# A fused attention and two-MLP kernel: a tile of ones is multiplied on TensorE behind the first q transposes and behind six score groups of pair 0

## The chip, the core and the metric

The kernel runs on one NeuronCore of one Trainium2 chip, in one launch. The metric is the device time of an execution in microseconds (us). Before the change three runs took 1049.36, 1034.11 and 1044.68 us, so their median is 1044.68 us. One more execution was profiled: it took 1044.74 us, and the span from its first to its last instruction is 1043.0 us, so 1.74 us lie outside what the trace shows.

## What is computed

In float32: attention over 4 batches and 8 heads with 576 positions of 64 numbers, then two feed-forward blocks over the 2304 resulting rows of 512.

```python
q_rot, k_rot = (rotate(q), rotate(k))            # rotary embedding, halves of 32
scores = scale * np.matmul(q_rot, k_rot.transpose(0, 1, 3, 2))
attn = np.exp(scores - np.max(scores, axis=-1, keepdims=True))
attn = attn / (np.sum(attn, axis=-1, keepdims=True) + 1e-09)
x = np.matmul(attn, v)                           # heads side by side: 2304 x 512
h = x @ w_in;  x = (h - np.tanh(h)) @ w_out      # 512 -> 2048 -> 512
x = ((x @ w1) * (x @ w2)) @ w3 @ w_o2            # 512 -> 1024 -> 1024 -> 512
```

## The kernel before, in words

**Pairs and steps.** Attention goes in 16 pairs of heads (4 batches x 4 pairs). A pair's q, k and v are loaded for two heads side by side, so that one 128x128 transpose serves both. Of the 576 positions, 512 are four chunks of 128, and the last 64 of both heads make a fifth chunk, the tails. So a pair has nine score groups (step S0 for the tails, S1 to S8 for four chunks x two heads), each a 128x576 tile.

**A score group's way through the engines.** TensorE multiplies a group (`score`, L535, PSUM tile `sc`, of which there are two buffers). VectorE takes the negated maximum of each row (`top`, L540, `nm`). ScalarE writes the exponentials with their sums (`exps`, L545, `e`), and that frees the `sc` buffer. VectorE inverts the sums, GpSimd divides (`norm`, L565), TensorE transposes the result in blocks (`trans`, L593 and L596, PSUM tile `te`), ScalarE and VectorE evict it (`eta`, `etb`, `ett`), and `pv` (L631, L634) multiplies with v.

**Before the scores of a pair** TensorE transposes the rotated k (`prep_k`, step KT, L454, `tk`), the tails (`prep_t`, TT, L460, `tt`) and q (`prep_q`, QT, L417, `tq`). ScalarE and VectorE split each into a rounded high part and the rest (`kp`: steps K1, K2, E1, ES; `qp`: Q1, Q2; `qtd`: G and H). For pair 0 the score matmuls read `kp` and `qp` in place: three terms for each half of the columns, six matmuls of 288 columns a group, whose operands fill 64 of 128 partitions; only S0 fills 128. For later pairs the SP queue copies `kp` and `qp` into stacked tiles `ks` and `qs` first (`twice_k` L504, steps KD0 to KD3, and `twice_q` L448, QD0 to QD3), and a group is four matmuls.

**Matmuls of ones.** `keep_busy` (L362) takes a PSUM buffer and multiplies a 128x128 tile of ones with itself `count` times. Nothing reads the result. In float32 each such matmul leaves two rows in the trace.

```python
def keep_busy(count):
    ps = psum.tile([128, 512], F32, tag="t", name="busy", bufs=4)
    for _ in range(count):
        nc.tensor.matmul(ps[:, 0:128], ones, ones, start=True, stop=True)
```

The PSUM tag "t" has four buffers, taken in turn, and `tk`, `tt`, `tq`, `te`, `pv` and the tiles of ones all take theirs from it. A tile of ones therefore waits for whatever held its buffer to be evicted, and moves the turn on by one for those behind it.

**What sets the order.** Every step has a name and a number: FIRST holds them for the first six pairs, DUE with a fixed period for the rest. WARM adds steps Z of pair 0, as (number, count of matmuls). All are sorted by number, and the instructions of each engine are issued in that sorted order; the numbers fix the order only, and no engine waits for a time. In pair 0, QT has the number 9685, S0 11161, S1 12531, KT of pair 1 13491, S2 14203, S3 15733, TT and QT of pair 1 16693 and 16854, S4 17405, S5 18935 and T0, the first transposes of exponentials, 19895 (Sn is score group n).

```python
todo_list += [(t, f"Z{c}", 0) for t, c in WARM]
todo_list.sort()
```

In the trace's names `sc<-kp,qtd` is group 0, `sc<-kp,qp` are the groups 1 to 8 of pair 0, and `sc<-ks,qs` are those of later pairs.

After attention the two feed-forward blocks follow, with weights that are converted from 64-bit floats beside the attention and beside the matmuls.

Of the kernel before, what the change touches and what calls it, by code (L numbers as in the profile page):

```python
# [202 lines left out]
EARLY = 12  # L203


WARM = [(0, 4), (1, 4), (2, 4), (3, 4), (7481, 6), (14204, 2), (16897, 1), (17406, 1)]


HI_SCALE = 2.0 ** -112
# [2 lines left out]
def fused_kernel(tc, q, k, v, w_in, w_out, w1, w2, w3, w_o2, tables, out):  # L212
# [516 lines left out]
    def perform(name, n):  # L729
# [66 lines left out]
        else:  # L796
# [7 lines left out]
                  for name, t in DUE.items()]  # L804
    todo_list += [(t, f"Z{c}", 0) for t, c in WARM]
    todo_list.sort()
# [408 lines left out]
```

## Time and profile before

| what | value |
|---|---|
| median of three runs | 1044.68 us (1034.11 to 1049.36) |
| profiled execution | 1044.74 us, span 1043.0 us |
| TensorE busy | 1031.0 us, 99% of the span |
| VectorE, ScalarE, GpSimd busy | 698.6, 610.6, 241.2 us |
| mean granted TensorE clock | 0.989 |
| share of TensorE in the chain that ended last | 88% |

TensorE's clock has two levels here: a granted clock of 1.0 is 2.4 GHz and one of 0.5 is 1.2 GHz. A line PEclk gives the granted share. Matmuls overlap each other in the trace, so the time that a group of them takes is read from its first start to the start of the next group. Idle time in brackets stands before an instruction, with what ended it.

### The profile page before, as it was taken

Reading aid. Unit: us, or ns where it says so; the run is one execution under the profiler, and the core shown is the slowest. Engines: PE = TensorE matmul, PEld = TensorE weight load, DVE = VectorE, ACT = ScalarE, POOL = GpSimd, SP = SyncE. Lnnn points to the kernel's source line nnn. Section 1 sums busy time; section 2 is a strip of 40 time slices with the busy share of each in tenths; the row PEclk is TensorE's granted clock in tenths of the full one; section 3 lists DMA queues with packets and bytes.
Section 4 is the critical chain, followed back from the end, with each engine's and each line's share of the span. In section 5 each row is a group of like instructions: output and inputs, shape, how many; then the busy total and the mean of one; then the engine's idle time right before and its main releaser. Section 6 shows DMA issues by size and latency. Waiting matters only on the chain.

```text
span 1043.0 us, 15833 instructions
## 1 busy us (share of the span) xinstructions
PE 1031.0 (99%) x5620; PEld 856.1 (82%) x5620; DVE 698.6 (67%) x1354; ACT 610.6 (59%) x1341; POOL 241.2 (23%) x292
## 2 busy tenths in 40 slices
PE   9999999999999999999999999999999999999998
PEld 7888788888777888898888888898888888888887
DVE  6799999999679877778998776798811212112121
ACT  3789898898778766577886666587511112112111
POOL 3577778777430000000000001100102003020000
PEclk7899999999999999999999999999999999999999
DMA  6477776776343533243434452530500101001010
GB/s 184 106 198 182 187 198 177 197 184 161 79 164 140 171 132 112 91 131 143 141 98 145 141 178 85 186 108 1 202 0 1 41 1 41 1 1 41 1 41 21
DMA packets 71326, 115.00 MB, mean 110 GB/s; under 512 B 12240, under 2 KB 42960, under 8 KB 71248
## 3 DMA queue, kind: packets, MB, share of 16 engines
q1 hardware_dynamic: 71088, 113.73, 36.6%
q8 instruction: 45, 0.74, 0.3%
q14 instruction: 33, 0.27, 0.1%
q10 hardware_dynamic: 160, 0.26, 0.1%
HBM read 67.96 MB, written 20.45 MB: 85 GB/s over the span
## 4 chain that ended last, share of the span: by engine, by line
PE 88%; DMA 4%; DVE 4%; ACT 2%; issue 1%; SPq 0%; POOL 0%; DVEq 0%; ACTq 0%
PE pw L1067 19%; PE x2p L916 17%; PE h L878 16%; PE o L1126 9%; PE sc L535 8%; PE te L593 5%; PE pv L634 5%; PE wp L963 4%; PE pv L631 1%; DMA qs<-qp 1%; PE te L596 1%; PE tw L948 1%; PE tq L417 1%; DMA raw_w<-in_moe_w 1%; DVE nm L540 1%
## 5 line engine op out<-in xcount | busy, mean ns | idle before, releaser
L916 PE MATMUL x2p<-g,s_out 128*128 128x512 f32 (+1 forms) x960 | 212.2, 369 | 2.0 <-DVE x L926 0.8
L916 PEld LDWEIGHTS x2p<-g,s_out 128*128 128x128 f32 x960 | 168.3, 188 | 34.0 <-ACT g L901 1.9
L1073 DVE TENSOR_TENSOR ab<-a,pw 128x512 f32<-128x512 f32 (+1 forms) x40 | 25.4, 635 | 195.5 <-PE pw L1067 195.5
L565 POOL TENSOR_SCALAR e<-e,r 128x576 f32<-128x576 f32 x144 | 113.8, 799 | 76.1 <-DVE r L561 62.0
L545 ACT ACTIVATE e<-sc,nm 128x576 f32<-128x576 f32 x144 | 107.5, 747 | 18.2 <-DVE nm L540 16.1
L540 DVE TENSOR_REDUCE nm<-sc 128x1 f32<-128x576 f32 x144 | 106.8, 750 | 14.5 <-PE sc L535 13.7
L878 PE MATMUL h<-xl,s_in 128*128 128x512 f32 (+1 forms) x480 | 106.8, 370 | 0.0
L1126 PE MATMUL o<-wpt,abs 128*128 128x512 f32 x432 | 104.5, 390 | 0.0
L1071 ACT COPY a<-pw 128x512 f32<-128x512 f32 (+1 forms) x40 | 21.8, 544 | 129.0 <-PE pw L1067 129.0
L878 PEld LDWEIGHTS h<-xl,s_in 128*128 128x128 f32 x480 | 83.7, 189 | 14.7
L975 POOL TENSOR_TENSOR wpe<-wpe 128x512 fp32r<-128x512 f32 x8 | 11.1, 1392 | 360.2 <-ACT wpe L974 360.2
L1126 PEld LDWEIGHTS o<-wpt,abs 128*128 128x128 f32 x432 | 80.6, 188 | 16.4
L535 PE MATMUL sc<-ks,qs 128*128 128x288 f32 x480 | 89.7, 316 | 2.8 <-ACT etb L620 1.7
L535 PEld LDWEIGHTS sc<-ks,qs 128*128 128x128 f32 x480 | 67.4, 189 | 18.4 <-ACT e L545 10.6
L895 DVE TENSOR_TENSOR g_s<-g_s,h 128x512 f32<-128x512 f32 (+1 forms) x80 | 50.6, 632 | 42.2 <-ACT g_m L894 42.1
L593 PE MATMUL te<-ident,e 128*128 128x128 f32 x576 | 78.6, 277 | 0.1
L1075 ACT CAST abs<-ab 128x512 fp32r<-128x512 f32 (+1 forms) x40 | 23.1, 577 | 94.3 <-DVE ab L1073 94.3
L891 ACT ACTIVATE g_s<-h 128x512 f32<-128x512 f32 (+1 forms) x80 | 44.3, 553 | 53.7 <-PE h L878 53.5
L901 ACT CAST g<-g_q 128x512 fp32r<-128x512 f32 (+1 forms) x80 | 46.2, 577 | 39.7 <-DVE g_q L898 39.2
L593 PEld LDWEIGHTS te<-ident,e 128*128 128x128 f32 x576 | 67.3, 143 | 1.9 <-issue 0.8
L902 DVE TENSOR_TENSOR g<-g_q,g 128x512 fp32r<-128x512 f32 (+1 forms) x80 | 50.7, 634 | 15.7 <-ACT g L901 15.1
L898 DVE COPY_PREDICATED g_q<-g_m,g_t 128x512 f32<-128x512 int32 (+1 forms) x80 | 56.5, 706 | 0.6
(306 smaller groups left out, 2093.2 us busy)
## 6 DMA issues: line engine op xcount, KB each, us to landing
ks<-kp SPq DMA_DIRECT2D x60, 288.0 KB, 4.1
raw_w<-in_moe_w SPq DMA_DIRECT2D x32, 512.0 KB, 4.1
raw_in<-in_moe_w_in SPq DMA_DIRECT2D x16, 512.0 KB, 3.8
raw_out<-in_moe_w_out SPq DMA_DIRECT2D x16, 512.0 KB, 3.6
xl<-xs_dram SPq DMA_DIRECT2D x16, 512.0 KB, 6.3
qs<-qp SPq DMA_DIRECT2D x60, 128.0 KB, 3.0
wp_dram<-wpe SPq DMA_DIRECT2D x24, 256.0 KB, 2.3
k<-in_k SPq DMA_DIRECT2D x16, 256.0 KB, 3.6
```

What stands on the lines that cost most here:

```text
L535: nc.tensor.matmul(s[:, n, 0:HS], lhs, rhs, start=t == 0, stop=t == len(terms) - 1)
L540: nc.vector.tensor_reduce(d["nm"][:, j:j + 1], d["ss"][j][:, :, 0:HS], AX.XY, ALU.max, negate=True)
L545: nc.scalar.activation(d["e"][:, j, :].rearrange("p (n s) -> p n s", n=2), d["ss"][j][:, :, 0:HS], AF.Exp, bias=d["nm"][:, j:j + 1], accum ...
L565: nc.gpsimd.tensor_scalar(d["e"][:, j, :], d["e"][:, j, :], d["r"][:, j:j + 1], 1.0, ALU.mult, ALU.mult)
L593: nc.tensor.transpose(ps[:, n * 128:(n + 1) * 128], e[:, o + n * 128:o + (n + 1) * 128], ident)
L634: nc.tensor.matmul(ps[64 * j:64 * j + 64, 0:n], vt[:, j, m, :], et[j][:, m, :], start=False, stop=m == NQ - 1, skip_group_check=True)
L878: nc.tensor.matmul(ps[:, 0:w], ws[:, a, kk], x[:, b_, 0:w], start=kc == 0 and t == 0, stop=kc == NK - 1 and t == 2)
L898: nc.vector.copy_predicated(qq, mk.bitcast(I32), t)
L902: nc.vector.tensor_tensor(g[:, 1, 0:w], qq, f32(g[:, 0, 0:w]), ALU.subtract))
L916: nc.tensor.matmul(x2ps[j][o][:, 0:w], ws[:, a, oo], g[:, b_, 0:w], start=c == 0 and t == 0, stop=c == HF - 1 and t == 2)
L1067: nc.tensor.matmul(ps[:, 0:w], ws[:, a, kk], x[:, b_, 0:w], start=kc == 0 and t == 0, stop=kc == NK - 1 and t == 2)
L1126: nc.tensor.matmul(outps[j][t], g[:, a, tt], wp[c][:, b_, :], start=c == 0 and i == 0, stop=c == NF2 - 1 and i == 2)
```

## The change

Only the table of the steps Z is another one. The first five entries (numbers 0 to 3 and 7481) are the same. The three behind them, with two, one and one matmuls, give way to seven: eight matmuls directly behind QT of pair 0, three behind each of S0, S1, S2, S3 and S4, and two behind S5. In all 25 matmuls of ones stand behind QT where there were 4.

```diff
-WARM = [(0, 4), (1, 4), (2, 4), (3, 4), (7481, 6), (14204, 2), (16897, 1), (17406, 1)]
+WARM = [(0, 4), (1, 4), (2, 4), (3, 4), (7481, 6), (9686, 8), (11162, 3), (12532, 3), (14204, 3), (15734, 3), (17406, 3), (18936, 2)]
```

TensorE's order behind the q transposes of pair 0 (`tq_0`), before the change; `sc_0` is group 0, the two `sc_1` are the two heads of the first chunk, `tk_1` is pair 1's k:

```order
L417 MATMUL tq_0_182<-ident,raq_0_148 128x128 x4
L535 MATMUL sc_0_205<-kp_0_172,qtd_96 128x288 x6
L535 MATMUL sc_1_219<-kp_0_172,qp_0_198 128x288 x6
L454 MATMUL tk_1_231<-ident,rak_1_175 128x128 x4
L535 MATMUL sc_1_240<-kp_0_172,qp_0_198 128x288 x6
L365 MATMUL busy<-ones 128x128 x2
```

The same place now:

```order
L417 MATMUL tq_0_182<-ident,raq_0_148 128x128 x4
L365 MATMUL busy<-ones 128x128 x8
L535 MATMUL sc_0_214<-kp_0_172,qtd_96 128x288 x6
L365 MATMUL busy<-ones 128x128 x3
L535 MATMUL sc_1_232<-kp_0_172,qp_0_207 128x288 x6
L365 MATMUL busy<-ones 128x128 x3
L454 MATMUL tk_1_248<-ident,rak_1_175 128x128 x4
L535 MATMUL sc_1_257<-kp_0_172,qp_0_207 128x288 x6
L365 MATMUL busy<-ones 128x128 x3
```

Group 0 now stands behind eight matmuls of ones, and the k transposes of pair 1 behind fourteen.

TensorE's order around the tails and q of pair 1 (`tt_1`, `tq_1`) up to the first transposes of exponentials, before:

```order
L535 MATMUL sc_2_261<-kp_0_172,qp_0_198 128x288 x6
L460 MATMUL tt_1_270<-ident,rt_167 128x128
L417 MATMUL tq_1_272<-ident,raq_1_226 128x128 x4
L365 MATMUL busy<-ones 128x128
L535 MATMUL sc_2_284<-kp_0_172,qp_0_198 128x288 x6
L365 MATMUL busy<-ones 128x128
L535 MATMUL sc_3_313<-kp_0_172,qp_0_198 128x288 x6
L593 MATMUL te_0_324<-ident,e_202 128x128 x4
```

And now:

```order
L535 MATMUL sc_2_279<-kp_0_172,qp_0_207 128x288 x6
L365 MATMUL busy<-ones 128x128 x3
L460 MATMUL tt_1_292<-ident,rt_167 128x128
L417 MATMUL tq_1_294<-ident,raq_1_243 128x128 x4
L535 MATMUL sc_2_304<-kp_0_172,qp_0_207 128x288 x6
L365 MATMUL busy<-ones 128x128 x3
L535 MATMUL sc_3_335<-kp_0_172,qp_0_207 128x288 x6
L365 MATMUL busy<-ones 128x128 x2
L593 MATMUL te_0_349<-ident,e_211 128x128 x4
```

The transposes of pair 1 moved behind three more matmuls of ones, and the ones end directly ahead of the first `te`. The order on VectorE, ScalarE, GpSimd and the SP queue is the same as before.

## Rows read from the trace of the kernel before

**Rows 1.** The page's span in 40 equal slices: granted clock in tenths.

```profile
PEclk7899999999999999999999999999999999999999
```

**Rows 2.** Windows: start:end us, length, busy us (count) by engine, granted clock, DMA share, GB/s.

```profile
7.00:10.00 3.00, 2.97 (x27) 2.79 (x26) 2.96 (x9) 0.72 (x2) 0.00 (x0) 1.00 1.01 342
10.00:13.70 3.70, 3.03 (x17) 2.00 (x16) 3.66 (x11) 1.26 (x5) 1.28 (x1) 1.00 1.05 336
14.30:34.20 19.90, 19.90 (x74) 16.57 (x74) 11.03 (x26) 10.46 (x29) 7.67 (x11) 0.50 0.52 127
34.00:35.00 1.00, 1.00 (x7) 0.85 (x7) 0.45 (x1) 0.00 (x0) 1.00 (x2) 0.89 0.00 0
47.70:51.50 3.80, 3.80 (x32) 3.50 (x30) 3.61 (x10) 3.76 (x12) 2.71 (x4) 1.00 1.00 243
60.00:80.00 20.00, 20.00 (x154) 15.70 (x152) 19.41 (x48) 17.73 (x51) 14.49 (x17) 1.00 0.68 172
10.00:34.40 24.40, 23.73 (x93) 18.92 (x91) 15.29 (x38) 12.32 (x35) 9.56 (x12) 0.58 0.59 157
```

**Rows 3.** Timeline of TensorE, pair 0: start us, us, operation, xcount [idle before <-releaser].

```profile
7.99 1.50 PE L365 MATMUL busy<-ones 128*128 128x128 f32 x12
9.66 0.60 PE L417 MATMUL tq<-ident,raq 128*128 128x128 f32 x4
10.34 0.53 PE L535 MATMUL sc<-kp,qtd 128*128 128x288 f32 x2
11.19 0.80 PE L535 MATMUL sc<-kp,qtd 128*128 128x288 f32 x4 [0.32 <-DVE qtd L493]
...
17.14 1.81 PE L535 MATMUL sc<-kp,qp 64*128 64x288 f32 x6
18.88 0.47 PE L460 MATMUL tt<-ident,rt 128*128 128x128 f32 x1
...
34.44 1.06 PE L535 MATMUL sc<-kp,qtd 128*128 128x288 f32 x6
```

**Rows 4.** Timeline of TensorE in a later pair, at the full clock.

```profile
51.56 1.06 PE L535 MATMUL sc<-kp,qtd 128*128 128x288 f32 x6
52.47 0.60 PE L454 MATMUL tk<-ident,rak 128*128 128x128 f32 x4
52.90 0.60 PE L593 MATMUL te<-ident,e 128*128 128x128 f32 x4
```

**Rows 5.** TensorE's groups by line from 47.7 to 51.5 us.

```profile
L593 PE MATMUL te<-ident,e 128*128 128x128 f32 x20 | 2.7, 275 | 0.0
L535 PE MATMUL sc<-ks,qs 128*128 128x288 f32 x9 | 1.9, 318 | 0.0
```

**Rows 6.** VectorE: one row of its waits from 14 to 34.4 us (total, times, longest); its timeline.

```profile
DVE nm L540 <- PE sc L535: 7.1, 6, 1.5
...
19.90 0.29 DVE L484 TENSOR_TENSOR kp<-tt,kp 128x128 fp32r<-128x128 f32 x1 [0.16 <-ACT kp L482]
```

**Rows 7.** SP queue's issues for pair 1, then landing times of qs and of ks.

```profile
20.23 2.20 SPq L504 DMA_DIRECT2D ks<-kp  x3
22.53 3.44 SPq L448 DMA_DIRECT2D qs<-qp  x3
26.01 0.62 SPq L504 DMA_DIRECT2D ks<-kp  x1
26.67 0.60 SPq L448 DMA_DIRECT2D qs<-qp  x1
...
DMA to landing us min/median/max: 2.9/3.7/4.8
...
DMA to landing us min/median/max: 3.6/4.1/5.1
```

**Rows 8.** Timeline of TensorE: the score matmuls that read those copies.

```profile
36.57 0.77 PE L535 MATMUL sc<-ks,qs 128*128 128x288 f32 x4
37.28 0.79 PE L535 MATMUL sc<-ks,qs 128*128 128x288 f32 x4
```

## The prediction

> **What bounds the kernel now.** I read the page's slices first. Every slice from the third on shows TensorE's granted clock at nine tenths or more; the first two show 7 and 8 [rows 1]. So whatever the clock can give back lies in the first 52 us. Windows cut finer place it: 1.00 from 10.0 to 13.7 us, 0.50 from 14.3 to 34.2, and 0.89 in the us from 34.0 [rows 2]. That is one stretch of some 20 us at 1.2 GHz, and 2.4 GHz from then on. The profiled execution took 1044.74 us, 0.06 above the median of the three runs, so the sum stands against either.
>
> In this stretch TensorE is the bound: busy 19.90 of 19.90 us, with VectorE at 11.03, ScalarE at 10.46 and GpSimd at 7.67 [rows 2]. VectorE's row of waits says the same from the other side: it waited six times, 7.1 us in all, for a score group [rows 6]. What TensorE did before the clock fell is in two windows: 2.97 of 3.00 us busy from 7 to 10, then 3.03 of 3.70 from 10.0 to 13.7 [rows 2], where the first scores wait for `kp`, `qtd` and `qp`. The latter window holds the only long holes ahead of the fall. I take the holes to be the cause; the trace shows the order of the two, not the cause. The eight new matmuls fill exactly these holes.
>
> **What the change adds and what it frees.** Only TensorE's order changes. I need its work from pair 0's q transposes to pair 1's first scores, which took from 9.66 to 34.44 us [rows 3], with every piece at the full clock.
>
> - A matmul of ones: 12 trace rows took 1.50 us [rows 3]. With the last one's own length of about 0.27 (the mean of a 128-column row [rows 5]) taken off, eleven steps make 1.23, 0.112 each. A matmul has two rows, so 0.224 us. 25 of them: 5.6 us, of which the 4 old ones were 0.9.
> - A score group of six matmuls: 51.56 to 52.47, 0.91 us [rows 4]; at the low clock 17.14 to 18.88, 1.74 [rows 3]. Nine groups: 8.2 us.
> - A transpose: 52.47 to 52.90 for four, 0.11 each [rows 4]. In the path stand 4 of q, 4 of pair 1's k, 5 of its tails and q, and 19 of exponentials: 32, so 3.5 us.
>
> The sum is 17.3 us, so pair 1's scores start at 9.66 + 17.3 = 27.0 in place of 34.44: 7.4 us earlier. The ones are on this path in full, since TensorE has next to no hole left in it. Without any of them the work would be 11.7 us, and other engines would bound it.
>
> Can they follow? VectorE's work from 10.0 to 34.4 is 15.29 us [rows 2], so it can't be done with that before 25.3: a gain of 9.1 us is the ceiling, and at 27.0 VectorE is busy nine tenths of the time. ScalarE (12.32) and GpSimd (9.56) have more room. The loop of two score buffers doesn't bind: VectorE's maximum and ScalarE's exponentials work on one group while TensorE fills the other, and a group with three ones behind it takes TensorE 0.91 + 0.67 = 1.58 us.
>
> Group 0 is delayed. It began at 10.34 [rows 3]; now eight ones, 1.8 us, stand ahead of it from about 10.1 on, so it begins near 11.9 and ends near 12.8, some 0.8 later than before (11.19 + 0.80 [rows 3]). The holes took the rest, and the sum has this in it.
>
> Next in the chain are pair 1's copies. The first was issued at 20.23, right behind `kp` on VectorE (19.90), which follows the tails' transpose at 18.88 [rows 3, 6, 7]. In the new order that transpose has ahead of it 20 ones, four groups, and 8 transposes: 4.5 + 3.6 + 0.9 behind 9.66 gives 18.7. So it moves by 0.2, and its and q's own run at the full clock gives perhaps 0.4 more. The SP queue then needed 7 us for eight issues, the last at 26.67 [rows 7]. At a landing time of 3.7 (qs) and 4.1 (ks) the last two landed near 30.1 and 30.4, where TensorE read them at 36.57 and 37.28 [rows 7, 8]: 6 us of cover. Moved by 0.5 they land near 29.6 and 29.9, while TensorE would want them at 29.1 and 29.9. The cover is gone: between nothing and, with the longest landings (5.1 and 4.8), 1.5 us are lost. I take 0.6, near the medians.
>
> **The tiles of ones turn the four PSUM buffers on.** The transposes of the tails' exponentials then need the buffer that pair 1's q held, and one group of ones needs the one that its k held. Both are evicted by VectorE work that has TensorE's next-but-one group behind it; I cost this at nothing, under the cover of 1.58 us for a group.
>
> **Sum:** 1044.74 - 7.4 + 0.6 = 1037.9 us; I say **1038**. From 60 to 80 us TensorE is busy 20.00 of 20.00 [rows 2], so what is earlier at 34 us should stay earlier.
>
> A rule that speaks against this: from 47.7 to 51.5 us TensorE's work was 20 block transposes of exponentials and 9 score matmuls, and the clock stayed at 1.00 [rows 2, 5]. The Trainium skill, "TensorE: Matmul & The Clock Gate", section "Part 4: PE-mode transpose", says that transposes do not count as busy work for the clock. This trace does not bear that out, at least where the clock is already up. By the rule the sum would end at the third rival's time.
>
> **The rivals.**
>
> 1. *The clock falls all the same, and the ones then cost their full price: slower.* TensorE has no hole at the low clock, and a matmul of ones takes twice 0.224 there, 0.45. If the clock fell where it did, 14 of the ones would be over, partly in the holes (about 1 us net), and 11 in place of 4 would follow: 7 x 0.45 = 3.1. That gives 1048.8. If it fell near 10, 21 more at 0.45 give 9.4, so 1054. It decides if the clock is at 0.50 in any window from 11 to 20 us. Against it: the holes are filled, and the fall followed them.
> 2. *Nothing in the end: 1044 to 1046.* The clock stays up, but the copies, or VectorE, which is busy 19.41 of 20 us later on [rows 2], give the time back by the end of attention; or the clock falls for only part of the stretch. Against the first: TensorE waited for nobody between 60 and 80 us.
> 3. *The clock falls once the ones end.* The last stand ahead of the first transposes of exponentials. Behind them, up to 34.44, come 19 transposes and three groups whose operands fill but 64 partitions. At the full clock that is 19 x 0.11 + 3 x 0.91 = 4.8 us, at the low one about twice that. A fall soon after would cost 3 to 5 us: 1041 to 1043. For it: the rule above, and the half-filled groups. Against it: the transposes from 47.7 on.
>
> **How the numbers follow.** The forecast, the clock up throughout, has 0.68. The slower rival has 0.11, the "nothing" 0.09, the late fall 0.12. The unknown costs reach from 1036 (no copy late) to 1040 (copies late by 1.5 and VectorE behind), and from VectorE's ceiling 1035.6 at the least. One of the three runs before took 1034.11, 10.6 below the profiled one; that would fit an execution in which the clock did not fall, but there is no trace of it. It puts a floor under what the clock can give. Range: **1034 to 1046**, which holds the forecast, the late fall and most of "nothing", and leaves out the slower rival.
>
> About 2% (21 us) is what a measurement of this kernel can tell from no change. No case comes near it: the whole of the clock's loss is some 10 us and the dearest rival costs 9.4. Faster by over 2%: 0.02. Within: 0.96. Slower: 0.02.
>
> **What would show it.** In the changed profile: the granted clock at 1.00 from about 7 us on with no window at 0.50; group 0 starting near 12; pair 1's first scores near 27; and ahead of the first `sc<-ks,qs` a wait of up to 1 us for a copy of `ks` or `qs`, which was not there. The step that is weakest is the first: if a window between 11 and 30 us stands at 0.50, the prediction is wrong by what that window holds. If the clock stays up and pair 1 starts near 27 but the span is not shorter, the loss is behind 34 us.

## The result and the profile after: the clock holds, and the kernel is 0.9% slower

Twenty runs of each kernel: 1038.72 us median before (1034.11 to 1052.57), 1049.65 after (1046.02 to 1052.72). The ratio is 1.0089, 95% interval 1.0065 to 1.0113. The prediction said 1038 in a range of 1034 to 1046: the median is outside of it and on the other side. The profiled execution of after took 1047.79 us. One execution in the experiments below, the tenth of e11, took 1456.43 us at a mean granted clock of 0.652 and is left out of every comparison.

The pages of after and of before, their instruction counts and the granted clock by slices:

```profile
span 1046.0 us, 15917 instructions
PEclk9999999999999999999999999999999999999999
```

```profile
span 1043.0 us, 15833 instructions
```

The first two slices of the clock, at 7 and 8 tenths in before [rows 1], are now nines. The second thing to see is that the program has 84 more instructions: 21 more matmuls of ones, each four rows (two weight loads, two matmuls). The prediction counted their time and nothing else.

TensorE's timeline of pair 0, after:

```profile
10.12 1.95 PE L365 MATMUL busy<-ones 128*128 128x128 f32 x16
11.82 1.05 PE L535 MATMUL sc<-kp,qtd 128*128 128x288 f32 x6
12.71 0.83 PE L365 MATMUL busy<-ones 128*128 128x128 f32 x6
13.47 1.06 PE L535 MATMUL sc<-kp,qp 64*128 64x288 f32 x6
14.46 0.94 PE L365 MATMUL busy<-ones 128*128 128x128 f32 x6
...
28.81 1.06 PE L535 MATMUL sc<-kp,qtd 128*128 128x288 f32 x6
...
30.94 0.78 PE L535 MATMUL sc<-ks,qs 128*128 128x288 f32 x4
```

Group 0 begins at 11.82 (forecast: near 11.9) and pair 1 at 28.81 in place of 34.44 [rows 3]: 5.6 us earlier (forecast: 7.4). The first group that reads pair 1's copies begins at 30.94 with no idle time ahead of it, so the 0.6 us put down for them was not lost.

Then the gain goes. Windows from pair to pair (start:end, length, busy us by engine, clock, DMA share, GB/s), first of after, then pair 8 of before:

```profile
10.00:28.81 18.81, 18.81 (x135) 16.31 (x133) 15.25 (x38) 11.34 (x34) 8.97 (x11) 1.00 0.59 152
28.81:62.13 33.32, 33.28 (x253) 26.89 (x252) 31.31 (x75) 28.16 (x80) 23.26 (x29) 1.00 0.66 162
...
131.75:149.87 18.12, 16.92 (x127) 13.33 (x124) 16.32 (x40) 14.62 (x41) 12.49 (x16) 1.00 0.66 169
149.87:167.93 18.06, 16.96 (x127) 13.34 (x125) 16.64 (x40) 14.72 (x41) 12.41 (x16) 1.00 0.67 170
```

```profile
151.35:167.94 16.59, 16.59 (x126) 13.33 (x125) 15.78 (x40) 14.65 (x41) 12.54 (x16) 1.00 0.73 185
```

Up to 62 us after is 5.6 us ahead (before reaches the same pair at 67.69). Some of its pairs then take 18.0 to 18.1 us, at the same clock of 1.00: pair 4 (17.1 in before) and pairs 6 to 11 (16.6 to 16.8 in before). TensorE is idle for some 1.1 us in each, with the same work in it. By 167.93 the two stand level (before: 167.94), and at the end after is 3.0 us behind. Behind attention nothing differs: from the last attention matmul to the end 749.6 us after, 750.0 before.

**Two kinds of execution of before.** Of 95 further runs of before (12 by themselves, 83 beside other kernels), 62 have a mean granted clock of 0.998 or more and take 1036.6 us median (1034.1 to 1044.3); 33 have 0.986 to 0.992 and take 1045.9 (1043.1 to 1049.6). All twenty of after have 0.999 or 1.0. The profiled execution of before was of the rarer kind. At the same clock the change costs 1049.7 - 1036.6 = 13 us.

### The profile page after: what moved, and what is told of

Its sections match the earlier page's. It is cut to its first block, busy times and chain, and to the rows that moved or that the text cites. A ratio compares the mean times of both kernels' runs of the same rounds, so it can differ in the third digit from the quotient of the medians.

```text
span 1046.0 us, 15917 instructions
## 1 busy us (share of the span) xinstructions
PE 1028.1 (98%) x5662; PEld 852.7 (82%) x5662; DVE 703.4 (67%) x1354; ACT 610.2 (58%) x1341; POOL 240.2 (23%) x292
## 4 chain that ended last, share of the span: by engine, by line
PE 79%; DVE 7%; ACT 6%; POOL 3%; DMA 3%; issue 2%; SPq 0%; ACTq 0%; DVEq 0%; POOLq 0%
PE pw L1067 19%; PE x2p L916 17%; PE h L878 17%; PE o L1126 9%; PE wp L963 4%; PE sc L535 4%; PE pv L634 3%; PE te L593 2%; ACT e L545 2%; DVE nm L540 2%; POOL e L565 1%; POOL raq L392 1%; PE busy L365 1%; PE tw L948 1%; PE pv L631 1%
```

## Where one slow pair loses its time

Pair 8 starts at 149.87 in after and at 151.35 in before. TensorE's timeline there, after and then before:

```profile
149.87 1.06 PE L535 MATMUL sc<-kp,qtd 128*128 128x288 f32 x6
...
151.64 0.27 PE L596 MATMUL te<-ident,e 128*128 128x128 f32 x1
152.34 0.77 PE L535 MATMUL sc<-ks,qs 128*128 128x288 f32 x4 [0.42 <-PE te L596]
...
156.11 1.30 PE L535 MATMUL sc<-ks,qs 128*128 128x288 f32 x8 [0.16 <-DMA qs<-qp]
...
160.32 0.30 PE L460 MATMUL tt<-ident,rt 128*128 128x128 f32 x1 [0.51 <-POOL e L565]
```

```profile
151.35 1.06 PE L535 MATMUL sc<-kp,qtd 128*128 128x288 f32 x6
...
153.22 0.79 PE L535 MATMUL sc<-ks,qs 128*128 128x288 f32 x4
...
156.78 1.34 PE L535 MATMUL sc<-ks,qs 128*128 128x288 f32 x8
...
160.35 0.27 PE L460 MATMUL tt<-ident,rt 128*128 128x128 f32 x1
```

Counted from the pair's start, the first `sc<-ks,qs` begins at 2.47 and not at 1.87 (0.60 late), the next at 6.24 and not 5.43 (0.81), the tails' transpose `tt` at 10.45 and not 9.00 (1.45). That is nearly the whole of the pair's 1.47 us. The 0.21 between the first two is a wait for another copy of `qs`, which the row at 156.11 names.

*The first 0.60.* The releaser named there is TensorE's own `te`, which had long been done, so it was something else. The copy of `qs` that this group reads: first its issue and landing time after, then before (each the one issue in a window of 0.5 us):

```profile
L448 SPq DMA_DIRECT2D qs<-qp x1: 547/547/547, 148.5 to 148.5; - x1
...
DMA to landing us min/median/max: 3.6/3.6/3.6
```

```profile
L448 SPq DMA_DIRECT2D qs<-qp x1: 543/543/543, 149.9 to 149.9; - x1
...
DMA to landing us min/median/max: 2.3/2.3/2.3
```

It was issued 1.3 us ahead of the pair's start in after, 1.45 in before, and landed at +2.27 and at +0.87. Before had 1.0 us of cover there; the copy is now 1.3 us slower, and TensorE's group starts 0.2 us behind the landing. The DMA queues in the 3.6 us from 1.7 ahead of the start to 1.9 behind it, after and then before:

```profile
q1 hardware_dynamic: 398, 0.56, 68.7%
q8 instruction: 1, 0.02, 2.0%
```

```profile
q1 hardware_dynamic: 457, 0.69, 86.2%
```

One packet of 16 KB on q8, a queue of instructions, stands in that stretch of after and none in before. Its 2.0% is a share of 16 engines' 3.6 us, so the packet took 1.15 us, nearly as long as the copy is late. (The lower share of q1, 68.7% against 86.2%, says nothing of this: less was issued in that stretch, 0.56 MB against 0.69.) There are 45 such packets in either kernel, one for every 252 of after's 2 x 5662 TensorE rows. I take them for TensorE's fetches, since they move when TensorE's instructions alone change (e5 and e10 below). A pair has 126 matmuls and 125 weight loads (the windows above), so about one fetch falls into each pair, and 84 more rows ahead of pair 1 should move it by a third of a pair, by this estimate some 5.5 us earlier. The Trainium skill, "Runtime: NRT & Kernel Launch", section "Instruction fetch mechanics", says that each engine's sequencer fetches its instructions through a DMA queue of its own in blocks of 16 KiB, 256 instructions, and that this is mostly hidden. The packets' size and number agree; hidden it is from TensorE itself (e4 below), but not from the copies.

*The last 0.64.* VectorE's and GpSimd's timelines show it (after, then before):

```profile
158.26 1.31 DVE L385 TENSOR_TENSOR rak<-k,tab 128x256 f32<-128x256 f32 x1
...
158.01 1.27 POOL L718 TENSOR_TENSOR s_out<-z_out,s_out 128x512 fp32r<-128x512 f32 x1
```

```profile
158.96 0.45 DVE L385 TENSOR_TENSOR rak<-k,tab 128x256 f32<-128x256 f32 x1
...
159.69 1.28 POOL L718 TENSOR_TENSOR s_out<-z_out,s_out 128x512 fp32r<-128x512 f32 x1
```

VectorE's step comes 0.8 us later in the pair, now falls beside GpSimd's subtract (step c4, the weights' low part), and takes 1.31 us in place of 0.45. It ends 0.3 us behind that subtract; in before it stood beside a smaller step of GpSimd.

Where the fetches fall, worked out from the trace's packets of q8 (us after the pair's first scores), with each pair's length:

```
pair                  1     2     3     4     5     6     7     8     9    10    11
before   fetch      9.9  10.2  10.3  10.4   8.4   8.0   8.3   6.6   6.1   6.0   4.0
         length    17.1  16.1  16.6  17.1  16.6  16.8  16.6  16.6  16.6  16.6  16.6
after    fetch      4.0   6.4   6.0   3.8   5.4   2.8  -0.1  -0.2   0.5  -0.1   0.1
         length    17.1  16.2  16.7  18.0  16.8  18.1  18.1  18.1  18.1  18.1  18.1
```

From pair 1 to 7 it moved by 3.0 to 8.4 us, 5.3 in the mean. Pair 4 of after doesn't fit: no fetch stands near its start, and e7 below shows the same pair as slow without the change.

The traces of all nine kernels in which the load of `vbd` has its old place (before, after, e1 to e3, e5 to e7, e10) give the same copy of pairs 4 to 14 in 99 cases, worked out from the packets of q8 and the landing times. In 30 a packet of q8 is in flight beside it, and 29 of these took 3.1 to 4.2 us; in 69 there is none, and 66 of these took 2.3 to 2.7 (the other three, pair 14 of e3, e6 and e10, 2.9 to 3.2). So the fetch and the late copy go together; the experiments had to show what moves the fetch.

## The experiments

Each kernel was timed beside runs of before, whose median was 1038.28, 1037.26 and 1039.22 us on the three occasions. Edits to the table of steps change one step's due time.

**The kernel before again, by itself (e1, e7).** No edit.

> The kernel before, again, for its spread: its runs lie at 1034 to 1039 us and at 1044 to 1052 us. If the low clock of pair 0 is what parts the two groups, every run near 1036 has a mean granted clock of about 1.00 and every run over 1044 one of about 0.99. If it is the pair period of attention (16.6 or 18.1 us), then some runs over 1044 have a clock of 1.00, and the profile's period tells which of the two that run has.

Measured: 1037.36 us median of 12 (1034.13 to 1047.97), ratio 0.9977 [0.994, 1.0013]. Two runs at a mean clock of 0.987 and 0.988 took 1045.94 and 1047.97, ten at 0.998 or more 1034.1 to 1038.6: the clock parts them. The profile caught one of the two.

> The kernel before once more, for a trace of an execution whose clock stays up, if it is one (about three in five are): pair 1 then starts at 26 to 28 us, without any of the ones behind q, and the periods are 16.6 us.

Measured: one run, 1035.49 us, mean clock 1.0. Windows of its first stretch and of pair 4, TensorE's timeline of pair 0:

```profile
10.00:25.84 15.84, 15.01 (x95) 11.65 (x92) 14.88 (x38) 11.45 (x34) 8.89 (x11) 1.00 0.66 172
75.69:93.76 18.07, 16.70 (x127) 13.27 (x125) 16.34 (x40) 14.78 (x42) 12.50 (x16) 1.00 0.68 172
```

```profile
11.28 0.80 PE L535 MATMUL sc<-kp,qtd 128*128 128x288 f32 x4 [0.32 <-DVE qtd L493]
...
12.81 0.78 PE L535 MATMUL sc<-kp,qp 64*128 64x288 f32 x4 [0.27 <-DVE qp L437]
```

The holes that I took for the cause of the fall are here as well, as long as in [rows 3] (0.32), and the clock did not fall. Pair 1 starts at 25.84. So in about two of three executions the old kernel needs no help, and there the ones are 3.0 us of plain delay (28.81 - 25.84). From pair 1 to the last attention matmul this execution took 258.2 us; after took 267.6. That is the other 9.4 us. Pair 4 is no part of it: it takes 18.07 us here too, with its fetch 11.5 us behind its start. Pairs 6 to 11, six times 1.5 us, are nearly all of it.

**One group made late (e2).** In before, four matmuls ahead of the first group of pair 6's copies:

```diff
+        if (i, j) == (6 * (NQ + 1) + 1, 0):
+            for _ in range(4):
+                nc.tensor.matmul(s[:, 0, 0:128], ident, ident, start=True, stop=True)
```

> The kernel before, with four matmuls of the identity (0.9 us of TensorE) ahead of the second score group of pair 6, into that group's own buffer: one delay of 0.9 us in the steady part of attention, nothing else. Theory of the loop (one late score group puts VectorE's rotation of k under GpSimd's conversion, that makes the copies of the next pair late, and so on): the periods of the pairs 6 to 12 become 18.0 us, and the time rises by 7 to 10 us over an execution of the kernel before with 16.6. Rival (a late group costs itself alone): 0.9 us at pair 6, then 16.6 again.

Measured: 1048.76 us (1038.37 to 1052.07, 10 runs), ratio 1.0071 [1.0026, 1.0115]. Seven of the ten had the lower clock (1047.9 to 1052.1), so the median says little; three at 1.00 took 1038.4 to 1041.1. The windows of pairs 5, 6 and 7 tell more:

```profile
103.96:120.54 16.58, 16.58 (x127) 13.34 (x125) 15.79 (x40) 14.64 (x41) 12.57 (x16) 1.00 0.74 187
120.54:138.64 18.10, 17.67 (x134) 14.18 (x133) 16.54 (x40) 14.63 (x41) 12.47 (x16) 1.00 0.74 183
138.64:155.23 16.59, 16.59 (x127) 13.33 (x125) 15.79 (x40) 14.63 (x41) 12.57 (x16) 1.00 0.71 186
```

A group made 0.9 us late costs its pair 1.5 us, and the next pair is at 16.59 again. A late group doesn't keep itself going from pair to pair; something in after makes the group late anew each time.

**GpSimd's subtract moved away from VectorE's step (e3)**, after with the step c4 due 2 us later, in DUE as shown here and in five tables of FIRST:

```diff
-    ... "c3": 26881, "W1": 29718, "c4": 41366,
+    ... "c3": 26881, "W1": 29718, "c4": 43366,
```

> The changed kernel, with GpSimd's low-part conversion of a weight (s_in, s_out, 1.28 us) behind the next division of exponentials instead of ahead of it, in every pair; TensorE, VectorE, ScalarE and SP unchanged. Theory of the loop: VectorE's k rotation no longer takes 1.19 us, the pairs 4 to 12 stay near 16.6 us, and the time falls from 1049.7 to 1036 to 1040. Rival (the copies are late because of the transfers' own time, whatever GpSimd does): periods stay at 18.0 and the time at 1047 to 1052.

Measured: 1045.83 us (1043.79 to 1050.35, 10 runs), ratio 1.0051 [1.0015, 1.0087]. Neither forecast came true: pairs 7, 8, 10 and 11 take 17.55 to 17.58 us, and pairs 6 and 9, where the step meets the moved subtract, 18.8. In pair 8 VectorE's step is down to 0.59 us and ends 9.2 us into the pair in place of 9.7; half a us a pair comes back and 1 us stays. The collision is a link of the chain and not its head.

**The queue ahead of the q copies cleared (e4)**: the load of `vbd` (step VB1), which stands right ahead of them on the SP queue, put ahead of the k copies; after with the following in DUE, and the same in three tables of FIRST:

```diff
-    ... "X5": 12423, "S6": 12455, "VB1": 12523, "N3": 12742,
+    ... "X5": 12423, "S6": 12455, "VB1": 9323, "N3": 12742,
```

> The changed kernel, with the small load of v (vbd, 1.36 us of the SP queue) issued ahead of the copies of k and not between those of k and q, from pair 3 on. If the SP queue's time ahead of the q copies is what makes the second score group late, the copies come 1.3 us earlier, the pairs 4 to 12 stay at 16.6 us and the time is 1036 to 1040. If the collision on VectorE alone sustains it, whatever the copies do, the periods stay at 18 and the time at 1047 to 1052.

Measured: 1042.91 us (1038.71 to 1045.84, 10 runs), ratio 1.0026 [0.999, 1.0062]. Window of pair 8; the copy that its first group reads; DMA queues in the same 3.6 us as above:

```profile
146.86:163.45 16.59, 16.59 (x126) 13.31 (x125) 15.79 (x40) 14.74 (x41) 12.58 (x16) 1.00 0.70 185
```

```profile
L448 SPq DMA_DIRECT2D qs<-qp x1: 1330/1330/1330, 144.2 to 144.2; - x1
...
DMA to landing us min/median/max: 3.5/3.5/3.5
```

```profile
q1 hardware_dynamic: 422, 0.77, 89.8%
q8 instruction: 1, 0.02, 1.6%
```

The fetch still falls into nearly the same place (0.3 us behind the start), but the copy is issued at -2.70 and lands at +0.75, and the pair takes 16.59. Its 3.5 us are not the fetch's work: in e8, with the same early load and no fetch there, it takes 3.5 as well. The fetch now meets the copy behind it, which lands in 4.0 us in place of 2.7 in e8, and nothing waits for that one. So the fetch doesn't starve TensorE; it costs only through a copy that has no cover. The median missed the 1036 to 1040 of the forecast: pairs 6 and 13 were still slow (18.07, 17.81), pair 13 with a fetch 0.3 us ahead of its start, and pair 6 where its second group waited 1.0 us for a later copy, which a fetch at 3.7 us met.

**The same ones in half the instructions (e5)**, after with

```diff
-    ones = att.tile([128, 128], F32, tag="e", name="ones", bufs=E_BUFS)
+    ones = att.tile([128, 512], F32R, tag="e", name="ones", bufs=E_BUFS)
...
-            nc.tensor.matmul(ps[:, 0:128], ones, ones, start=True, stop=True)
+            nc.tensor.matmul(ps, ones[:, 0:128], ones, start=True, stop=True)
```

> The changed kernel, every matmul of ones as one pass over 512 columns (fp32r) instead of four cycles a column over 128 (float32): the same TensorE time, 0.21 us, and half the instructions, so that attention begins 94 instructions of TensorE earlier in its stream than in the changed kernel and 10 earlier than in the kernel before. Theory of the fetches (TensorE's instruction fetches of 16 KB, about one a pair, fall into the copies of q at the start of the pairs 6 to 12 because the ones shifted them): the fetches return to 10 us into pair 3 and 4 to 8 us into the pairs 6 to 11, the periods to 16.6, the granted clock stays at 1.00, and the time is 1036 to 1041. Rival (the early start of pair 1, or the waits among the ones, set the slow periods): 18.0 again and 1047 to 1052.

Measured: 1039.91 us (1038.23 to 1041.25, 10 runs), ratio 0.9993 [0.9959, 1.0026]; clock 0.999 or 1.0 in all ten. **Each of these matmuls as two halves (e10)**, e5 with

```diff
-            nc.tensor.matmul(ps, ones[:, 0:128], ones, start=True, stop=True)
+            for m in (slice(0, 256), slice(256, 512)):
+                nc.tensor.matmul(ps[:, m], ones[:, 0:128], ones[:, m], start=True, stop=True)
```

> The control of the one-pass run: the changed kernel with the same fp32r ones, but each matmul as two of 256 columns, so that the time on TensorE is again the same and the instructions are as many as in the changed kernel (four trace rows for each matmul of ones, 84 more than before). Theory of the fetches: the slow periods of 18.05 us come back in the pairs 4 to 11 and the time is 1047 to 1052. Rival (fp32r in place of float32 cured it): 1038 to 1041.

Measured: 1050.09 us (1047.96 to 1051.68, 10 runs), ratio 1.0078 [1.0043, 1.0113]; clock 0.999 or 1.0. Pairs 6 to 10 and 12 take 18.0 to 18.3 us; in e5 they take 16.6. The two kernels side by side, first e5, then e10: window of pair 8, landing of the copy, queues.

```profile
147.50:164.09 16.59, 16.59 (x127) 13.32 (x125) 15.78 (x40) 14.66 (x41) 12.54 (x16) 1.00 0.73 185
```

```profile
DMA to landing us min/median/max: 2.3/2.3/2.3
```

```profile
150.91:168.97 18.06, 16.82 (x126) 13.30 (x125) 16.05 (x40) 14.61 (x41) 12.43 (x16) 1.00 0.67 169
```

```profile
DMA to landing us min/median/max: 4.0/4.0/4.0
```

```profile
q1 hardware_dynamic: 395, 0.55, 69.7%
q8 instruction: 1, 0.02, 2.6%
```

In e5 no packet of q8 stands in that stretch (it falls at +6.1, in e10 at -0.1). Both give pair 0 the same columns of ones at the same clock, and pair 1 starts at 29.38 and 29.53. They differ by one weight load and one matmul for each, and by 10.2 us, the 10 us that after loses against e5. (They were timed on two occasions; before's executions without the fall took 1036.8 us median on the first and 1036.5 on the second.) This is the run that settles it: not the time of the ones, nor their type, but how many instructions stand ahead of attention. A number that carries the fetch past the copies again was not tried.

**The instructions alone, in before (e6)**: 21 of the ones ahead of group 0 as two matmuls of 64 columns each.

```diff
+        halves = {4: 4, 6: 5}.get(count, 0)
+        for _ in range(2 * halves):
+            nc.tensor.matmul(ps[:, 0:64], ones, ones[:, 0:64], start=True, stop=True)
+        for _ in range(count - halves):
             nc.tensor.matmul(ps[:, 0:128], ones, ones, start=True, stop=True)
```

> The kernel before with its own WARM table, but of the 22 matmuls of ones ahead of the q transposes 21 are done as two halves of 64 columns: the same columns, 84 instructions of TensorE more, exactly as many as the change adds. Theory of the fetches: the pairs 6 to 12 take 18.0 us as in the changed kernel, and executions whose clock stays up take 1045 to 1050 instead of 1034 to 1039. Rival (the ones behind q matter by what they do, not by their number): 1034 to 1039 with the clock up, as before.

Measured: 1058.22 us (1056.39 to 1058.56, 4 runs), ratio 1.0168 [1.0101, 1.0235]. It was meant to take no time of its own, and that failed, as two rows of TensorE show.

```profile
1.05 13.91 PE L366 MATMUL busy<-ones 128*128 128x64 f32 x64 [1.05 <-DVE ones L360]
...
15.61 4.37 PE L366 MATMUL busy<-ones 128*128 128x64 f32 x20
```

64 rows in 13.91 us are 0.217 each; in before the first 32 rows of whole ones took 6.62 us, 0.207 each. But the 20 half rows at 15.61 still took 0.22 each, where whole ones in before took 0.112 from 7.99 us on [rows 3], and group 0 behind them took 1.9 us (21.24 to 23.15) in place of 0.9, all with the granted clock at 1.00. So TensorE as a whole kept the slow pace of the start for longer; the reason is open. Everything starts 10.6 us later than in e7 (pair 1 at 36.45). From there to the last attention matmul it took 269.7 us, as after (267.6) and not as before (258.2), with pairs 4 to 11 at 18.03 to 18.08 and fetches between -0.4 and 0.6 in pairs 7 to 11. So the same loss appears without any new ones behind q, but the run is not a clean one.

**e5 with the vbd load early (e8), before with it (e11)**, the edit of e4.

> The one-pass ones together with the early small load of v. Theory: the copies of q have 1.3 us of cover, so that no fetch makes a group late; the time is 1035 to 1039 with a clock of 1.00 in every execution, below the median of the kernel before (1038.3), which is a mix of two clocks. If the early load brings nothing once the fetches are out of the way, it equals the run with one-pass ones alone.

> The kernel before with the early small load of v alone. With the clock up it saves the one period of 18.07 us at pair 4: 1034 to 1037 in place of 1035 to 1039; executions with the low clock stay 9 us above that.

Measured: e8 1038.0 us (1036.06 to 1039.48, 10 runs), ratio 0.9991 [0.9964, 1.0017]. e11: of the nine other runs seven had the lower clock and took 1041.8 to 1044.6, two the upper and took 1034.79 and 1034.42; ratio 0.999 [0.9948, 1.0032]. At either clock that is some 2 us less than before, with but two runs at the upper one, and e8 is 1.9 less than e5. Pair 4, the one slow pair that the old program has at the upper clock (18.07 in e7), is at 16.46 in e11 and 16.48 in e8.

**Fewer ones, in one pass, with the vbd load early (e9)**, e8 with

```diff
-WARM = [..., (7481, 6), (9686, 8), (11162, 3), (12532, 3), (14204, 3), (15734, 3), (17406, 3), (18936, 2)]
+WARM = [..., (7481, 6), (9686, 5), (12532, 2), (14204, 2), (16897, 1), (17406, 1)]
```

> Towards a better kernel: the table of the kernel before plus five matmuls of ones behind q and two behind the second score group of pair 0, all as one pass of 512 columns, and the small load of v ahead of the copies of k. If seven matmuls fill enough of the holes, the clock stays up in every execution, pair 1 starts near 27 us, the periods are 16.6 and the time is 1034 to 1037, below both kernels. If they don't, part of the executions have a clock of 0.99 and take 9 us more.

Measured: 1035.56 us (1034.34 to 1038.49, 12 runs), ratio 0.995 [0.9918, 0.9982]: 0.5% less than before with its two clocks, and 0.9 us less than before's executions without the fall on that occasion (1036.5 median). The clock is 0.998 to 1.0 in all twelve, and windows of the profiled one show next to no idle time of TensorE in pair 0 and none in pair 8:

```profile
10.00:26.16 16.16, 16.09 (x98) 12.51 (x95) 15.03 (x38) 11.50 (x34) 8.89 (x11) 1.00 0.63 165
143.37:159.94 16.57, 16.57 (x127) 13.35 (x125) 15.77 (x40) 14.62 (x41) 12.52 (x16) 1.00 0.71 186
```

Seven more ones, ahead of pair 0's third score group, beside the four later ones that before has too, cost 0.3 us against the best case of before (pair 1 at 26.16 against 25.84).

## Why the prediction was wrong, point by point

**The step that failed** is the last sentence of the sum: TensorE was busy 20.00 of 20.00 us from 60 to 80 [rows 2], "so what is earlier at 34 us should stay earlier". A busy engine in one kernel's trace says that its operands came in time at the places where they stood; it doesn't say how near they were to coming late. The copy that pair 8's first group reads had 1.0 us of cover, and nothing in the sum asked for it. Behind it stands a costing at nothing that the prediction does not even name: 84 more instructions were charged with their time on TensorE and not with what they shift. The prediction's check named the outcome (pair 1 early, span not shorter: the loss is behind 34 us); rival 2 had the place of such a loss, the copies of later pairs, and put its price at the gain itself, 1044 to 1046. It was 9 us, more than the gain. e5 against e10 shows the cause, e4 the way it acts: through the copy's cover. What is not shown is why a fetch of 16 KB makes a copy of 128 KB land 1.3 us later. The packet's own 1.15 us is near that, which would fit a copy of which one part stands behind the packet on the same DMA engine, but the trace doesn't tell on which engine a packet went, and nothing was tried.

**The baseline.** The sum stood against 1044.74, an execution with the fall, while 62 of 95 runs have none. The prediction saw the sign (one run at 1034.11) and took it for a floor under the gain, not for the common case. Against the common case the ones could only lose: 3.0 us in pair 0. The forecast of 1037.9 was itself near what the change gives without the added instructions, 1039.9 in e5.

**The clock.** Forecast to stay up: it did, in all twenty runs. The reason given, the holes from 10.0 to 13.7 us, is only half of it: e7 has the holes and no fall, so they alone don't bring it. With ones behind the q transposes it never fell, in 82 executions of after, e3 to e5 and e8 to e10; so the ones keep the clock up. Why it falls in one run of three without them stays open, as does why in e2 and e11, whose pair 0 is that of before, it fell in seven of ten and seven of nine. Rival 1 (it falls all the same) and rival 3 (it falls once the ones end) did not come about. The rule of the Trainium skill, "TensorE: Matmul & The Clock Gate", "Part 4: PE-mode transpose", by which transposes do not count as busy work, was one ground of rival 3; the clock stayed at 1.00 from 28.81 us to the end of attention, with 50 transposes among some 126 matmul rows of pair 8. Nothing here bears the rule out, but score and `pv` matmuls stand between the transposes, so nothing here refutes it either.

**Sizes.** Pair 1 was 1.8 us later than the 27.0 of the sum. A group of six with 64 partitions takes 0.99 us (13.47 to 14.46), not the 0.91 of a full group in [rows 4]; with three ones behind it 1.76 (13.47 to 15.23) to 1.86 in place of 1.58. Three ones behind a group take 0.76 (12.71 to 13.47) to 0.87, not 0.67. Eight of them ahead of group 0 took 1.70 (10.12 to 11.82), near the 1.8 forecast. The cover of the first copies was not gone: TensorE came 1.8 us later than assumed to them, and they cost nothing.

## What to carry to other kernels

Count the instructions that a change adds ahead of a tight loop, and not only their time: where the loop's small copies land with a microsecond of cover or less, look up in the trace where the instruction queue's packets fall within one turn of the loop, and give the copies more cover (an earlier issue) before anything else. Where the effect to be removed shows in one execution, look first in how many others it shows: here the mean granted clock of each told them apart. And do filler work in the fewest instructions, here one pass of 512 columns (two trace rows, with its weight load) in place of one float32 matmul of 128 (four).

## What the runs showed of the hardware that was not expected

- One instruction fetch of 16 KB, at 1 to 3% of the DMA engines' time, made the on-chip copy of 128 KB beside it land in 3.6 to 4.0 us in place of 2.3 to 2.7, in pairs 7 to 11; with pair 6, where it stood beside a later copy (4.9 us in place of 4.0 in e5), that is 9 us of a kernel. Two fetches of 8 KB on the other instruction queue (q14) stand 1.5 us ahead of and 0.5 us behind the start of before's pair 9: there the copy took 2.7 us, still had its cover, and the pair took 16.57.
- A matmul of ones on float32 with 64 columns took 0.217 us a row at the program's start, no less than one with 128 there (0.207). In e6 that pace lasted to some 20 us, while before's rows were down to 0.112 us from 8 us on, at a granted clock of 1.00 in both.
- VectorE's multiply of 128x256 took 0.45 us in before, beside a smaller step of GpSimd. Where it started under GpSimd's subtract of 128x512, in pairs 8 to 11 of after, it took 1.19 to 1.38 us and ended 0.3 us behind that subtract.
- The same program, from the same start, had a mean granted clock of 0.986 to 0.992 in 33 of 95 executions (where one was traced, a fall of some 20 us) and of 0.998 or more in 62.
